# FFT filter and soft mixture of experts on one core: sign changes, row softmax, column maximum and first combine transposes placed elsewhere

## The chip, the cores and the metric

The kernel runs on one core of a Trainium2 chip. The metric is the device time of one execution in microseconds (us). The core has TensorE (PE in the profile; its weight loads are PEld), VectorE (DVE), ScalarE (ACT), GpSimd (POOL) and SyncE (SP, which here issues every DMA). Each engine works through a queue of its own in order, and waits at the head of that queue until what the next instruction needs is there.

## The reference

Two parts, one after the other. First a filter in the frequency domain, over the sequence of 2496, for 8 batches of 256 channels:

```
X = np.fft.rfft(x, axis=1)                # x: (8, 2496, 256)
Y = X * (filt_r + 1j * filt_i)[None]
y = np.fft.irfft(Y, n=2496, axis=1)
```

Then a soft mixture of experts over all 19968 tokens (8 experts, 4 slots each, hidden size 1024). It uses a softmax over tokens (down a column) to fill the 32 slots, and a softmax over slots (along a row) to give the slots' outputs back:

```
logits = x @ phi                          # (19968, 32)
d = softmax(logits, axis=0)               # per slot, over the tokens
slot_input = d.T @ x                      # (32, 256)
slot_out[e] = relu(slot_input[e] @ w1[e]) @ w2[e]
c = softmax(logits, axis=1)               # per token, over the slots
out = c @ slot_out
```

## The kernel before, in words

The transform of length 2496 is split into 39 x 64. For a batch b, eleven **s1 units** (`s1_unit`, L317) take the first transform. Each multiplies a tile of x with a table in three matmuls (L324); to keep precision x is split into a high part `xh` (ACT, L313) and a low part `xl` (POOL, L314). ACT copies the result to `at` (L325) and SP stores it in DRAM as `a_dram` (L329, L331, L332). Ten **x units** per batch (`x_unit`, L348) load it back in another layout as `ash` (L345), do the second transform (PE, L355) and multiply with the filter: DVE forms `yt` and `t2` with the tables `fr_t` and `fi_t` (L368, L369), and two half-size additions finish the complex product, L371 on DVE (on POOL for the last two batches) and L372 on POOL. Ten **t units** per batch (`t_unit`, L374) transpose the product (L380), copy it to `y` (ACT, L382), and matmul it with phi (L393) for the logits in the frequency domain, `lt` (L400). Batch 0 goes another way at the front: `first_unit` (L274) and `turn_ash` (L290) keep it on the chip.

The loop over 80 slots (L739, ten per batch) traces x units, s1 units of a batch some slots ahead, and t units. When x of batch 1 is loaded, three buffers of `xt` hold it (XB = 3); a buffer is free for the next load when its split by ACT and POOL is over.

**The tables.** `load_tables(c)` (L646) loads the parts of `fr_t` and `fi_t` for two residues t and changes the sign of some column runs of `fi_t` in place, on POOL (L653). There are ten such calls. The first four (c = 0 to 3) are traced before the first unit; the other six come in the first six slots of the loop. There are 29 sign changes: 11 in the first four calls, 18 in the other six.

**The chain of a group.** Two batches make a group g (0 to 3). When its last t unit is traced, `chain(g)` (L414) starts. It turns the logits back to the token domain (L444 to L491), takes the maximum of each slot over the group's tokens (L485, L498) in `cmax`, transposes that (L501), reduces it (L503), puts it on a diagonal `dg` (L505) and spreads it over all partitions with a matmul against `ones` (L508). This gives `m_run`. Then come the exponentials of the column softmax (L522, L523), their transform back to frequencies (L538 to L572), the sum of the exponentials `z` (L583, added in L593 or L598 as `z_ins`), and the sum over tokens `s` (80 matmuls, L604, added in L614 or L618). Last in program order is the **row softmax**: maximum along the rows `rm` (two DVE reductions, L626), subtraction and exponential in place (L630 on DVE, L631 on ACT), row sums `r_all` (L638) and their reciprocal (L640, L641). Groups 0 and 1 then store the exponentials to DRAM (`c_dram`, L644), since groups 0 to 2 share one buffer; they are read back near the end (L791).

**The order of work.** The program is traced in this order, but a list scheduler sets each engine's queue: it takes what is ready first by its own model of the times, and program order decides only among what is ready. So the row softmax, last in program order, may be issued long before `z`. `tc.issue_after(ins)` holds that back: what the block traces on `ins`'s engine is queued behind `ins`, without waiting for it to finish. In the kernel before, L620 does so for group 3 only. Group 2 is special: it is stopped before its `z` (L579) and its `s` matmuls are queued at given points of group 3's chain.

**The end.** After group 3, `psi` (L800, four matmuls) and `sit` (L802) give the slot inputs; then the experts (L865 to L891), and the combine. `combine(pos)` (L814) multiplies the exponentials with the reciprocal sums on POOL (`c1`, L826, and `cq`, L828 to L833), transposes them on PE (`ct`, L837, L840, L841) and splits them in two parts (L811 on ACT, L812 on DVE). The first one, `combine(0)`, is queued on PE behind `psi` (L854). It takes its PSUM tiles from the pool `ps_c`, which has two buffers and also holds `psi`; later ones use `ps_t`. The output matmuls (L918), the copies (L927) and the stores (L944) follow.

Of the kernel before, what the change touches and what calls it, by code (L numbers as in the profile page):

```python
# [9 lines left out]
F32 = mybir.dt.float32  # L10
F32R = mybir.dt.float32r
AF = mybir.ActivationFunctionType
ALU = mybir.AluOpType
AX = mybir.AxisListType
# [9 lines left out]
KR = PK * N1  # L24
# [11 lines left out]
SLOTS = NE * SPE  # L36
GROUPS = ((0, 1), (2, 3), (4, 5), (6, 7))
NG = len(GROUPS)
NSPILL = 2
OUT_ORDER = (4, 5, 0, 1, 2, 3, 6, 7)  # L40
P = 128
# [7 lines left out]
XB = 3  # L49
# [122 lines left out]
def flip_runs(t):  # L172

    out = []
    for c in range(N2):
        if bin_of(t, c) > SEQ // 2:
            if out and out[-1][1] == c:
                out[-1] = (out[-1][0], c + 1)
            else:
                out.append((c, c + 1))  # L180
    return out
# [27 lines left out]
def fft_soft_moe(ctx, tc, x, fr, fi, phi, w1, w2, cst, w1q, out):  # L209
    nc = tc.nc  # L210
    pe, dve, act, pool_e, sp = nc.tensor, nc.vector, nc.scalar, nc.gpsimd, nc.sync

    const = ctx.enter_context(tc.tile_pool(name="const", bufs=1))
# [14 lines left out]
    phi_t = const.tile([P, 2, SLOTS], F32, name="phi_t")  # L228
    r_all = const.tile([KR, NG, 4 * NH], F32, name="r_all")
    s_run = const.tile([P, DIM + 1], F32, name="s_run")  # L230
    cmax = const.tile([KR, SLOTS], F32, name="cmax")
    ones = const.tile([SLOTS, P], F32, name="ones")
    m_run = [const.tile([P, SLOTS], F32, name=f"m_run{i}") for i in range(NG)]

    def C(name, lo=0, hi=None):
        o, rows, cols = OFF[name]
        hi = cols if hi is None else hi
        return cst_t[0:rows, o + lo : o + hi]

    ident = C("id")  # L240

    def open_pool(name, bufs, side):
        cm = tc.tile_pool(name=name, bufs=bufs, side=side, reuse_waits="tile")
        return cm, cm.__enter__()
# [5 lines left out]
    warm_ins = dve.memset(warm, 0.0)  # L250
    with tc.issue_after(warm_ins.ins):
        nc.vector.memset(ones, 1.0)
    x0_cm, x0p = open_pool("x0p", 6, "left")
    tabs_cm, tabs = open_pool("tabs", 1, "right")
    prod_cm, prod = open_pool("prod", 2, "right")
# [148 lines left out]
    lgs = {}  # L404

    mark = {}

    def behind(g, n):

        if g != NG - 2:  # L410
            return nullcontext()
        return tc.issue_after(mark[g + 1, sum(n >= k for k in HELD)])

    def chain(g):  # L414
        bs = GROUPS[g]
        wk = late_pool[0] if g == NG - 1 else work
# [13 lines left out]
        def psum(shape, name):  # L430
            pool, tag = banks[turn[0] % len(banks)]
            turn[0] += 1
            return pool.tile(shape, F32, tag=tag, name=name)
# [36 lines left out]
        cm = wk.tile([KR, 3, SLOTS], F32, tag="cm", name=f"cm_{g}", bufs=1)  # L470
# [10 lines left out]
        for s0 in range(0, NH, SA):  # L481
# [4 lines left out]
                out=cm[:, s0 // SA, :],  # L486
                in_=pv[:, 0:n].rearrange("s a (x e) -> s e (a x)", e=SLOTS),
                axis=AX.X,
                op=ALU.max,
# [4 lines left out]
        nch = -(-NH // SA)  # L494

        NX = 2 * nb * NH
        lgf = lg_t.rearrange("s a h b e -> s (a h b) e")
        dve.tensor_reduce(out=cmax, in_=cm[:, 0:nch].rearrange("s c e -> s e c"), axis=AX.X, op=ALU.max)  # L498
        m_new, m_old = m_run[g], m_run[g - 1]
        pm = psum([SLOTS, KR], f"mt_{g}")  # L500
        mark[g, 1] = pe.transpose(pm, cmax, ident[0:KR, 0:KR]).ins  # L501
        mx = wk.tile([SLOTS, 1], F32, tag="mx", name=f"mx_{g}", bufs=1)
        dve.tensor_reduce(out=mx, in_=pm, axis=AX.X, op=ALU.max)  # L503
        dg = wk.tile([SLOTS, SLOTS], F32, tag="dg", name=f"dg_{g}", bufs=1)
        dve.tensor_scalar(out=dg, in0=ident[0:SLOTS, 0:SLOTS], scalar1=mx, scalar2=None, op0=ALU.mult)  # L505
        yield
        pmb = psum([P, SLOTS], f"mb_{g}")
        mark[g, 2] = pe.matmul(pmb, ones, dg, start=True, stop=True).ins  # L508
# [51 lines left out]
        for t0 in range(0, HT, SA):  # L560
# [10 lines left out]
            if t0 == 0:  # L571
                dve.tensor_scalar(  # L572
                    out=dd[:, 0, 0], in0=dd[:, 0, 0], scalar1=C("wh"), scalar2=None, op0=ALU.mult
# [12 lines left out]
        if g > 0:  # L586
# [6 lines left out]
            z_ins = dve.scalar_tensor_tensor(  # L593
                out=s_run[:, DIM:], in0=s_run[:, DIM:], scalar=alc, in1=pz, op0=ALU.mult, op1=ALU.add
            )
        else:
            alc = None
            z_ins = dve.tensor_copy(s_run[:, DIM:], pz)  # L598
        pss = psum([P, DIM], f"s_{g}")
        for b2, b in enumerate(bs):  # L600
            for t in range(NT):
                j = t % 4
                with behind(g, b2 * NT + t):
                    pe.matmul(  # L604
                        pss[32 * j : 32 * j + 32, :],
                        dd[:, t % HT, t // HT, b2, :],
                        ys[b, t // 2][:, t % 2, :],
                        start=(b2 == 0 and t < 4),
                        stop=(b2 == nb - 1 and t >= NT - 4),
                    )  # L610
                if t % 8 == 7:
                    yield
        if g > 0:
            s_ins = dve.scalar_tensor_tensor(  # L614
                out=s_run[:, 0:DIM], in0=s_run[:, 0:DIM], scalar=alc, in1=pss, op0=ALU.mult, op1=ALU.add
# [1 line left out]
        else:  # L617
            dve.tensor_copy(s_run[:, 0:DIM], pss)  # L618

        with tc.issue_after(z_ins.ins) if g == NG - 1 else nullcontext():  # L620
            rm = wk.tile([KR, NX], F32, tag="rm", name=f"rm_{g}", bufs=1)
            rs = r_all[:, g, 0:NX]
            step = NX // 2
            for x0 in range(0, NX, step):
                sl = slice(x0, x0 + step)
                dve.tensor_reduce(out=rm[:, sl], in_=lgf[:, sl], axis=AX.X, op=ALU.max)  # L626
        rmb = rm.rearrange("s (x o) -> s x o", o=1).broadcast_to([KR, NX, SLOTS])
        for x0 in range(0, NX, step):
            sl = slice(x0, x0 + step)
# [6 lines left out]
        for x0 in range(0, NX, step):  # L636
            sl = slice(x0, x0 + step)
# [8 lines left out]
    def load_tables(c):  # L646
        lo, hi = 2 * c, 2 * c + 2
        sp.dma_start(fr_t[:, lo:hi], fr.rearrange("q (t h c) -> q t h c", h=2, c=64)[:, lo:hi])
        sp.dma_start(fi_t[:, lo:hi], fi.rearrange("q (t h c) -> q t h c", h=2, c=64)[:, lo:hi])
        for t in range(lo, hi):  # L650
            for c0, c1 in flip_runs(t) if t else ():
                sl = fi_t[:, t, :, c0:c1]
                pool_e.tensor_scalar(out=sl, in0=sl, scalar1=-1.0, scalar2=None, op0=ALU.mult)  # L653

    CPB = NT // 2
    NS = BATCH * CPB
# [23 lines left out]
    if WM:  # L680
        pw = ps_c.tile([P, P], F32, tag="c", name="warm_up")
        for k in range(WM):
            pe.matmul(pw, warm, warm, start=True, stop=True)
    tabs_next = iter(range(CPB))
    load_tables(next(tabs_next))
    sp.dma_start(phi_t, phi.rearrange("(h q) e -> q h e", q=P))
    for k in range(XB):
        next_x()
        load_tables(next(tabs_next))
# [49 lines left out]
    for n in range(NS + LT):  # L739
# [21 lines left out]
        if n >= LT:  # L761
            b, c = divmod(n - LT, CPB)
# [36 lines left out]
    for dh in range(2):  # L799
        psi_ins = nc.tensor.matmul(psi[:, dh, :], s_run[:, dh * P : (dh + 1) * P], repz, start=True, stop=True)  # L800
# [48 lines left out]
    def new_st(pos):  # L849
        pool = tail if pos % SB < 2 else late_pool[-1]  # L850
        return pool.tile([P, 2, SQ + P], F32R, tag="st", name=f"st_{pos}", bufs=2)

    sts = {pos: new_st(pos) for pos in range(2)}
    with tc.issue_after(psi_ins.ins):  # L854
        combine(0)

    po = ps_s1.tile([P, DIM], F32, tag="s1", name="slot_out")
# [73 lines left out]
    for pos in range(BATCH):  # L931
        off = SQ * pos % P
        for m in range((off + SQ) // P):
            cols.append((sts[pos], m * P))
            g, n = nout[0], len(cols)
# [49 lines left out]
```

## Time and profile before

| what | value |
|---|---|
| median of 3 runs (lowest to highest) | 385.86 us (382.42 to 387.18) |
| the profiled execution's own time | 384.92 us |
| its span, first to last instruction | 382.8 us |
| mean granted TensorE clock | 0.974 |
| busy: PE, PEld, DVE, ACT, POOL | 349.9, 281.8, 264.2, 209.6, 213.5 us |
| DMA: moved, mean rate | 103.57 MB, 271 GB/s |

The profiled execution is 2.1 us longer than its span; that part lies around the span and is not touched here. A busy PE in this profile is not PE at its peak, since matmuls overlap and their ends are modelled. So the stretches count in which PE, or another engine, is shown idle, and what ended that idle time. "TensorE clock" is the share of the full clock that was granted.

### The profile page before, as it was taken

The page shows a single profiled execution, that of the slowest core. Times are in us where ns is not written, and L with a number is a line of the kernel's source. Part 1 is how long each engine was busy: PE and PEld are TensorE (multiplying, and loading weights), DVE is VectorE, ACT ScalarE, POOL GpSimd, SP SyncE. Part 2 cuts the span into 40 slices and gives each one's busy share as a digit, 9 for nine tenths or more (in the row PEclk, how much of TensorE's full clock was granted, in tenths as well). Part 3 has the DMA queues.
Part 4 walks back from the last instruction along what each step waited for, and adds up shares of the span by engine and source line. Part 5 has one row for each costly group of instructions (what it writes and reads, how often), then busy time and mean ns, then how long its engine had stood idle before and what let it go on. Part 6 is the DMA issues. An engine that isn't in the chain of part 4 may idle for free.

```text
span 382.8 us, 10537 instructions
## 1 busy us (share of the span) xinstructions
PE 349.9 (91%) x4111; PEld 281.8 (74%) x4111; DVE 264.2 (69%) x444; ACT 209.6 (55%) x415; POOL 213.5 (56%) x258
## 2 busy tenths in 40 slices
PE   8998969999999899999999999999989999999920
PEld 8896758888888677888887869888666534788820
DVE  2486716969798995588799837899745741677740
ACT  3757656786557864664896624336443330566730
POOL 0499966998678586585699707556640002434000
PEclk9999979999999999999999999999999999999985
DMA  7998899999879799695887835352499996699996
GB/s 245 374 281 277 224 319 281 322 310 364 299 204 293 244 303 275 197 287 139 273 276 243 264 110 174 110 129 84 145 309 380 384 383 174 241 377 413 412 419 284
DMA packets 53523, 103.57 MB, mean 271 GB/s; under 512 B 5391, under 2 KB 25999, under 8 KB 51171
## 3 DMA queue, kind: packets, MB, share of 16 engines
q1 hardware_dynamic: 53475, 102.92, 80.1%
q8 instruction: 32, 0.52, 0.5%
q14 instruction: 16, 0.13, 0.1%
HBM read 62.78 MB, written 40.12 MB: 269 GB/s over the span
## 4 chain that ended last, share of the span: by engine, by line
PE 66%; DMA 10%; DVE 9%; POOL 5%; issue 3%; ACT 2%; SPq 1%; DVEq 0%; ACTq 0%; POOLq 0%
PE x L355 14%; PE s L324 10%; PE t L380 8%; PE out L918 6%; PE s L604 5%; DMA xt<-in_x 4%; PE l L393 4%; PE v L457 3%; PE lg L484 3%; DMA out<-ob 2%; PE dd L563 2%; DMA a_dram<-at 2%; POOL xl L314 2%; PE o L882 2%; PE h L865 2%
## 5 line engine op out<-in xcount | busy, mean ns | idle before, releaser
L314 POOL TENSOR_TENSOR xl<-xt,xh 117x512 fp32r<-117x512 f32 x77 | 105.5, 1381 | 26.9 <-ACT xh L313 20.7
L355 PE MATMUL x<-cst_t,ash 128*128 128x128 f32 x640 | 87.9, 281 | 3.7 <-DMA ash<-a_dram 1.1
L355 PEld LDWEIGHTS x<-cst_t,ash 128*128 128x128 f32 x640 | 81.3, 195 | 9.8 <-issue 2.8
L372 POOL TENSOR_TENSOR yt<-yt,t 128x256 f32<-128x256 f32 x80 | 67.7, 850 | 15.5 <-DVE t L369 15.0
L368 DVE TENSOR_TENSOR yt<-x,fr_t 128x512 f32<-128x512 f32 x80 | 54.6, 682 | 28.3 <-PE l L393 17.8
L382 ACT COPY y<-t 128x512 f32<-128x512 f32 x80 | 46.7, 591 | 37.0 <-PE t L380 36.5
L313 ACT CAST xh<-xt 117x512 fp32r<-117x512 f32 x77 | 47.5, 624 | 21.0 <-DMA xt<-in_x 9.8
L369 DVE TENSOR_TENSOR t<-x,fi_t 128x512 f32<-128x512 f32 x80 | 54.2, 678 | 2.5 <-POOL yt L372 2.4
L325 ACT COPY at<-s 120x512 f32<-120x512 f32 x77 | 45.3, 590 | 13.3 <-PE s L324 11.3
L380 PE MATMUL t<-cst_t,yt 128*128 128x128 f32 x320 | 49.3, 278 | 1.1 <-POOL yt L372 0.6
L371 DVE TENSOR_TENSOR yt<-yt,t 128x256 f32<-128x256 f32 x60 | 47.6, 809 | 0.6
L380 PEld LDWEIGHTS t<-cst_t,yt 128*128 128x128 f32 x320 | 38.2, 143 | 12.3 <-issue 5.2
L324 PE MATMUL s<-xh,w1h 117*120 117x512 f32 x77 | 36.1, 469 | 3.6 <-ACT at L325 3.0
L826 POOL TENSOR_TENSOR c<-cl,r_all 117x352 f32<-117x352 f32 x8 | 6.2, 798 | 50.4 <-DMA cl<-c_dram 40.6
L324 PE MATMUL s<-xl,w1h 117*120 117x512 f32 x77 | 33.0, 428 | 0.8 <-POOL xl L314 0.8
L324 PE MATMUL s<-xh,w1l 117*120 117x512 f32 x77 | 31.0, 402 | 0.0
L371 POOL TENSOR_TENSOR yt<-yt,t 128x256 f32<-128x256 f32 x20 | 15.6, 779 | 26.9 <-DVE t L369 20.6
L918 PE MATMUL out<-so_h,st 32*128 32x256 f32 x312 | 27.3, 307 | 1.0 <-ACT so_h L894 0.5
L927 ACT COPY ob<-out 128x512 f32<-128x512 f32 (+1 forms) x42 | 21.9, 560 | 11.3 <-PE out L918 8.3
L927 DVE COPY ob<-out 128x512 f32<-128x512 f32 (+1 forms) x42 | 25.2, 647 | 3.8 <-PE out L918 2.1
L918 PE MATMUL out<-so_l,st 32*128 32x256 f32 x312 | 25.3, 284 | 0.0
L918 PEld LDWEIGHTS out<-so_h,st 32*128 32x128 f32 x312 | 20.0, 183 | 4.4 <-DVE ob L927 1.2
(112 smaller groups left out, 522.7 us busy)
## 6 DMA issues: line engine op xcount, KB each, us to landing
out<-ob SPq DMA_DIRECT2D x18, 1024.0 KB, 8.4
xt<-in_x SPq DMA_DIRECT2D x35, 512.0 KB, 4.8
ash<-a_dram SPq DMA_DIRECT2D x70, 256.0 KB, 4.3
a_dram<-at SPq DMA_DIRECT2D x70, 240.0 KB, 4.1
w<-in_w SPq DMA_DIRECT2D x64, 256.0 KB, 5.3
xt<-in_x SPq DMA_DIRECT2D x18, 256.0 KB, 5.1
c_dram<-lg SPq DMA_DIRECT2D x2, 643.5 KB
cl<-c_dram SPq DMA_DIRECT2D x2, 643.5 KB
```

What stands on the lines that cost most here:

```text
L313: act.copy(xh, xs)
L314: pool_e.tensor_tensor(out=xl, in0=xs, in1=xh.bitcast(F32), op=ALU.subtract)
L324: pe.matmul(ps, w, xx, start=(n == 0), stop=(n == 2))
L355: pe.matmul(ps[:, 2 * k + dh].rearrange("q r c -> q (r c)"), ash[:, k, dh * P : (dh + 1) * P], C("b"), start=True, stop=True,)
L368: dve.tensor_tensor(out=yt, in0=ps, in1=frv, op=ALU.mult)
L369: dve.tensor_tensor(out=t2, in0=ps[:, :, ::-1, :], in1=fiv, op=ALU.mult)
L371: add.tensor_tensor(out=yt[:, :, 1, :], in0=yt[:, :, 1, :], in1=t2[:, :, 1, :], op=ALU.add)
L372: pool_e.tensor_tensor(out=yt[:, :, 0, :], in0=yt[:, :, 0, :], in1=t2[:, :, 0, :], op=ALU.subtract)
L380: pe.transpose(pt[:, k, dh, :], yt[:, c % 2, 2 * k + dh].rearrange("q r c -> q (r c)"), ident)
L382: act.copy(y, pt.rearrange("k p h d -> k p (h d)"))
L918: last_mm[0] = nc.tensor.matmul(prs[k][:, mm, :], st[q, n % 2, c0 : c0 + P], (so_h, so_l)[n // 2][q, :], start=(n == 0), stop=(n == 3),).ins
L927: copied[k % 2] = copy(ob[:, nm * k : nm * (k + 1), :], prs[k]).ins
```

## The change

Four edits.

- The sign changes of `fi_t` leave POOL: those of the first four calls (c <= 3) go to DVE, as the same instruction; those of the other six go to ACT, as a copy with scale -1.
- The row softmax of groups 0 and 1 is queued behind the group's `z_ins` on DVE, as that of group 3 was already. Group 2's is left free as before.
- The column maximum works on full tiles: `cmax` has 128 columns instead of 32, the transposed tile `pm` 128 rows, and `ones` and `dg` 128 rows. `cmax` and `dg` are now allocated once and set to zero at the start.
- The PE instructions of `combine(0)` are queued behind the last `s` matmul instead of behind `psi`. `last_s[0]` holds the last L604 matmul traced.

```diff
-    cmax = const.tile([KR, SLOTS], F32, name="cmax")
-    ones = const.tile([SLOTS, P], F32, name="ones")
+    cmax = const.tile([KR, P], F32, name="cmax")
+    dg = const.tile([P, SLOTS], F32, name="dg")
+    ones = const.tile([P, P], F32, name="ones")
...
         nc.vector.memset(ones, 1.0)
+        nc.vector.memset(cmax, 0.0)
+        nc.vector.memset(dg, 0.0)
...
-        dve.tensor_reduce(out=cmax, in_=cm[:, 0:nch].rearrange("s c e -> s e c"), axis=AX.X, op=ALU.max)
+        dve.tensor_reduce(out=cmax[:, 0:SLOTS], in_=cm[:, 0:nch].rearrange("s c e -> s e c"), axis=AX.X, op=ALU.max)
...
-        pm = psum([SLOTS, KR], f"mt_{g}")
+        pm = psum([P, KR], f"mt_{g}")
...
-        dve.tensor_reduce(out=mx, in_=pm, axis=AX.X, op=ALU.max)
-        dg = wk.tile([SLOTS, SLOTS], F32, tag="dg", name=f"dg_{g}", bufs=1)
-        dve.tensor_scalar(out=dg, in0=ident[0:SLOTS, 0:SLOTS], scalar1=mx, scalar2=None, op0=ALU.mult)
+        dve.tensor_reduce(out=mx, in_=pm[0:SLOTS], axis=AX.X, op=ALU.max)
+        dve.tensor_scalar(out=dg[0:SLOTS], in0=ident[0:SLOTS, 0:SLOTS], scalar1=mx, scalar2=None, op0=ALU.mult)
...
-                    pe.matmul(
+                    last_s[0] = pe.matmul(
...
-                    )
+                    ).ins
...
-        with tc.issue_after(z_ins.ins) if g == NG - 1 else nullcontext():
+        with tc.issue_after(z_ins.ins) if g != NG - 2 else nullcontext():
...
-                pool_e.tensor_scalar(out=sl, in0=sl, scalar1=-1.0, scalar2=None, op0=ALU.mult)
+                if c <= XB:
+                    dve.tensor_scalar(out=sl, in0=sl, scalar1=-1.0, scalar2=None, op0=ALU.mult)
+                else:
+                    act.activation(sl, sl, AF.Copy, scale=-1.0)
...
-    with tc.issue_after(psi_ins.ins):
+    with tc.issue_after(last_s[0]):
         combine(0)
```

More of the change, by code (lines that the diff above doesn't have):

```diff
@@ L406, in fft_soft_moe @@
     mark = {}
+    last_s = [None]
     def behind(g, n):
```

## The prediction

> **What bounds the kernel now.** I read the page first, then the busy times by stretch, then the chain that ended last, then the waits of the stretches where PE stands.
>
> ```profile
> PE 349.9 (91%) x4111; PEld 281.8 (74%) x4111; DVE 264.2 (69%) x444; ACT 209.6 (55%) x415; POOL 213.5 (56%) x258
> ```
>
> PE is busy in 91% of the span, no other engine above 69%. What PE has to do is hardly touched, so a gain can only come from PE's pauses and from stretches with a low clock. Busy time by stretch (start:end, length, then busy time and count of PE, PEld, DVE, ACT, POOL, granted clock, DMA share, GB/s):
>
> ```profile
> 12.00:20.00 8.00, 7.05 (x56) 6.23 (x55) 3.38 (x5) 5.77 (x10) 4.84 (x8) 1.00 1.04 366
> 20.00:28.00 8.00, 8.00 (x62) 7.33 (x61) 7.21 (x12) 4.18 (x8) 8.00 (x16) 1.00 0.90 266
> 28.00:36.00 8.00, 7.60 (x49) 5.82 (x47) 5.26 (x8) 6.52 (x13) 8.00 (x18) 1.00 0.88 306
> 36.00:44.00 8.00, 6.63 (x67) 5.28 (x68) 4.67 (x7) 4.67 (x9) 8.00 (x9) 1.00 0.70 200
> 44.00:54.00 10.00, 6.77 (x37) 4.87 (x36) 4.98 (x7) 6.96 (x13) 10.00 (x10) 0.91 0.95 290
> 54.00:60.00 6.00, 6.00 (x28) 5.30 (x27) 0.00 (x0) 1.48 (x3) 1.65 (x2) 0.59 0.98 338
> 60.00:115.00 55.00, 55.00 (x567) 47.47 (x567) 46.79 (x72) 37.67 (x74) 44.92 (x42) 1.00 0.90 295
> ```
>
> From 20 to 54 us POOL works without a pause, while PE loses 0.40 + 1.37 + 3.23 = 5.0 us from 28 to 54. Then PE runs at a clock of 0.59 for 6 us, which costs another 6 x 0.41 = 2.5 us. From 60 us on PE has no pause for 55 us. So the start is where time can be had: 7.5 us at most, and POOL is the full engine there. The DMA engines, though, are at 0.70 to 1.04 themselves. What the start waits for in the end is in the chain (start, length, what):
>
> ```profile
> 45.25 3.20 DMA a_dram<-at
> 48.54 4.51 DMA ash<-a_dram
> 53.18 3.75 PE x L355 x16
> ```
>
> Batch 1 must be stored and loaded back before its x units, and its last store leaves at 45.25.
>
> **The sign changes.** The rows of POOL's 29 sign changes (least, median, greatest ns; first and last start) and what POOL waited for before them; then the SP queue's waits up to 60 us and PE's from 12 to 54 us:
>
> ```profile
> L653 POOL TENSOR_SCALAR fi_t<-fi_t x29: 222/357/513, 13.4 to 35.9; 128x64 f32<-128x64 f32 x9, 128x4 f32<-128x4 f32 x2, 128x60 f32<-128x60 f32 x2, 128x50 f32<-128x50 f32 x2
> ```
>
> ```profile
>   DMA fi_t<-in_fi: 13.0, 1
> ```
>
> ```profile
> SPq L329 <- ACT at L325: 8.5, 7, 2.5
> SPq L271 <- POOL xl L314: 3.4, 3, 2.6
> ```
>
> ```profile
> PE s L324 <- ACT at L325: 3.0, 4, 1.1
> ```
>
> At the median POOL is freed of 29 x 0.357 = 10.4 us, all of it ahead of batch 1's last splits. SP waits 8.5 us for `at` and 3.4 us for `xl`, with the next x loads queued behind. So the splits, the buffers of x and the loads come forward together. POOL allows 10.4 us, PE has 7.5 to give, and the transfers set a third limit: from 20 to 54 us they are busy for 0.90 x 8 + 0.88 x 8 + 0.70 x 8 + 0.95 x 10 = 29.3 of 34 us. The same bytes at the share of 0.95 seen from 44 to 54 take 29.3 / 0.95 = 30.9 us: 3.1 us earlier. I take 3.1 us, since the transfers are the nearest limit, and half of the low clock's 2.5 us, 1.2, because the pause of PE in front of it shrinks but need not vanish. Together 4.3 us.
>
> What the receivers pay. The nearest row for an ACT sign change, of at most 64 columns, is a copy of 128 columns, and the nearest for DVE is the scaling of `dd`, of 64:
>
> ```profile
> L400 ACT COPY lt<-l 128x128 f32<-128x128 f32 x1 | 0.3, 266 | 0.2 <-PE l L393 0.2
> ```
>
> ```profile
> L572 DVE TENSOR_SCALAR dd<-dd,cst_t x4: 255/1022/1276, 144.1 to 299.1; 128x64 f32<-128x64 f32 x4
> ```
>
> ACT: at most 18 x 0.266 = 4.8 us. From 20 to 36 us it is free for 3.82 + 1.48 = 5.3 us, which covers them; without that cover PE, which waits for `at` already (3.0 us), would lose up to 4.8 us more. DVE: 11 at 0.255 is 2.8 us, and at 1.022 it is 11.2 us. It has 4.62 us free from 12 to 20 us and 0.79 from 20 to 28. The one at 299 us, where POOL does nothing, is the short one. With POOL eased I take 0.4 each (4.4 us, covered), and keep 11.2 us for the range: 11.2 - 5.4 = 5.8 us on the path. The term is **-4.3**, from -7.5 to +5.8.
>
> A rule speaks against this edit. The Trainium skill, page "GPSIMD Engine Reference", section "Key points", says that GpSimd shares its SBUF interfaces with VectorE and contends with DVE instructions in a two-port mode or with two SBUF inputs. By it each DVE sign change beside a split goes at the long end, and the start would not gain but lose. The row of L572 bears it out as to the spread; whether eleven fall beside splits no run here shows yet.
>
> **Row softmax behind z.** PE's waits from 115 to 136 us (group 0) and from 186 to 207 us (group 1):
>
> ```profile
> PE x L355 <- PE x L355: 1.0, 1, 1.0
> PE x L355 <- PE t L380: 0.6, 1, 0.6
> PE t L380 <- DVE yt L371: 0.5, 1, 0.5
> ```
>
> ```profile
> PE s L324 <- POOL xl L314: 0.8, 2, 0.5
> ```
>
> 2.1 + 0.8 = 2.9 us in all. The longest one, on DVE and then on PE:
>
> ```profile
> 127.36 1.04 DVE L630 TENSOR_TENSOR lg<-lg,rm 117x704 f32<-117x704 f32 x1
> 128.33 0.68 DVE L369 TENSOR_TENSOR t<-x,fi_t 128x512 f32<-128x512 f32 x1
> ```
>
> ```profile
> 129.11 1.13 PE L355 MATMUL x<-cst_t,ash 128*128 128x128 f32 x8 [0.98 <-PE x L355]
> ```
>
> The row softmax's L630 holds DVE until 128.40, the multiplication L369 behind it frees the PSUM buffer at 129.01, and PE goes on at 129.11. Behind z there is a hole for this work, because PE runs only `s` there:
>
> ```profile
> 154.08 0.42 DVE L618 COPY s_run<-s 128x256 f32<-128x256 f32 x1 [4.18 <-PE s L604]
> ```
>
> ```profile
> 224.91 0.48 DVE L614 SCALAR_TENSOR_TENSOR s_run<-s_run,alc,s 128x256 f32<-128x256 f32 x1 [4.13 <-PE s L604]
> ```
>
> ```profile
> L630 DVE TENSOR_TENSOR lg<-lg,rm 117x704 f32<-117x704 f32 x8 | 7.8, 986 | 0.0
> L626 DVE TENSOR_REDUCE rm<-lg 117x22 f32<-117x704 f32 x8 | 7.0, 880 | 0.8 <-ACT lg L491 0.8
> L638 DVE TENSOR_REDUCE r_all<-lg 117x22 f32<-117x704 f32 x8 | 6.9, 872 | 0.1
> ```
>
> Per group 2 x 0.880 + 2 x 0.986 = 3.7 us go into 4.1 to 4.2 idle ones. The sums, 2 x 0.872 = 1.7 us, come after `s` among the next multiplications; if they are not hidden there they cost 1.7 us. Behind the waiting `rm` only its own chain is queued. The stores to `c_dram` move with it on SP:
>
> ```profile
> L644 SPq DMA_DIRECT2D c_dram<-lg x2: 353/384/416, 132.4 to 203.4; - x2
> ```
>
> ```profile
> 243.23 0.86 PE lg L484 x2
> ```
>
> They would leave at about 155 and 226, and the loads queued behind them on SP wait if the exponentials are late. Group 1's buffer is written again only after group 2's L484, at 243, so 17 us are left for that store. Not all of the 2.9 us hangs on row softmax (group 1's waits are for POOL), so I take some two thirds: **-2.0**, from -2.9 to +1.7.
>
> **Full tiles for the maximum.** The work stays as it is in count; the weights get 128 columns.
>
> ```profile
> L508 PEld LDWEIGHTS mb<-dg,ones 32*128 32x128 f32 x8 | 1.2, 182 | 1.0 <-issue 0.8 <-DVE yt L368 0.2
> ```
>
> 0.8 us of idle stands before the spreading matmuls, of four groups. I take **-0.2**, from -0.8 to 0, as the neighbours hide most of it. The two memsets at the start find DVE waiting for the first table. The Trainium skill, "TensorEngine Tiling (Array Packing)", "Key Properties", says that a change of tiling mode drains TensorE. By it the full 0.8 us would go where the neighbours are full tiles, and the forecast would be 378.8.
>
> **First combine transposes.** DVE, then PE around psi, the two halves of the split as groups, and the first matmul of the experts:
>
> ```profile
> 304.37 0.48 DVE L614 SCALAR_TENSOR_TENSOR s_run<-s_run,alc,s 128x256 f32<-128x256 f32 x1 [0.52 <-PE s L604]
> 305.57 0.23 DVE L802 COPY sit<-psi 128x64 f32<-128x64 f32 x1 [0.72 <-PE psi L800]
> ```
>
> ```profile
> 304.90 0.63 PE L800 MATMUL psi<-repz,s_run 128*128 128x32 f32 x4 [0.60 <-DVE s_run L614]
> 305.37 0.60 PE L837 MATMUL ct<-cst_t,c 117*128 117x117 f32 x4
> ```
>
> ```profile
> L812 DVE TENSOR_TENSOR st<-ct,st 128x468 fp32r<-128x468 f32 x8 | 5.2, 645 | 1.9 <-ACT st L811 1.9
> ```
>
> ```profile
> L811 ACT CAST st<-ct 128x468 fp32r<-128x468 f32 x8 | 4.5, 564 | 1.7 <-PE ct L837 1.7
> ```
>
> ```profile
> 306.32 3.64 PE L865 MATMUL h<-w,sit 128*32 128x512 f32 x32
> ```
>
> Now L865 starts 0.5 us after `sit` is ready (305.80), because the transposes lie between, from 305.37 on. Put ahead they fill the 0.60 us in which PE waits for `s_run`; as all of them take 0.95 us, psi slips by up to 0.35. So at best the 0.5 us goes. But `ps_c` has two buffers: if the transposes take both, psi waits until the first is split by ACT and DVE, 0.56 + 0.65 = 1.2 us. The two ends nearly cancel, and I take **0.0**, from -0.5 to +1.2.
>
> **Sum.** -4.3 - 2.0 - 0.2 + 0.0 = -6.5 us on the profiled execution's 384.9 us (span 382.8 and 2.1 around it): 378.4. The median of the runs is 0.9 us above that execution, so **379.4 us**, 1.7% below 385.86.
>
> **Rivals.** (A) *The transfers hold the start.* Batch 1 comes no earlier, since the DMA share is 0.95 to 1.04 in the stretches on either side; against it stands 0.70 from 36 to 44 us. Only -2.2 is left: 383.7. (B) *POOL was the only limit.* PE's pauses and the low clock go in full, -7.5, and row softmax gives -2.9: with -0.5 from the rest -10.9, so 375.0. For it: POOL at 8.00 of 8 from 20 on. Against: the DMA share. (C) *Row softmax only moves.* Its subtractions meet POOL's splits in the new place too, and the sums delay the next batch: +1.7 in place of -2.0, so 383.1. (D) *DVE's sign changes become the bound*, the slower side: in DVE's queue, from 12 to 28 us, each waits for POOL and takes 1.02 us; the first multiplications of batch 0 come 5.8 us late and PE, in order, with them. With -2.2 from the rest +3.6: 389.5. It decides from (4.62 + 0.79) / 11 = 0.49 us for each sign change on. This is the outcome that the page on GpSimd would have.
>
> **How the numbers follow.** Forecast 0.41, A 0.18, B 0.21, C 0.12, D 0.08. About 2% is what a measurement of this kernel can tell from no change: below 378.1 is faster, above 393.6 slower. All of B and a third of the forecast's share lie below 378.1: 0.21 + 0.13 = 0.34; of D a quarter above 393.6, 0.02; the rest, 0.64, within. The range of 373.5 to 387.0 takes in B, the forecast, A and C and leaves out most of D; the forecast's own range is 376.5 to 382.
>
> **What would show it.** Right: POOL has pauses between 20 and 44 us, the last store of batch 1 leaves before 43 us, its first x unit starts at about 50 and the clock from 54 to 60 us is well above 0.59. L626 of groups 0 and 1 starts right behind L598 and L593, the idle 4.1 us before L618 and L614 is gone, and no wait of PE near 129 us names a buffer held by L369. DVE's sign changes take below 0.49 us each, and L865 starts no later behind L614 than now (306.32 - 304.37 = 1.95 us). Wrong: x units of batch 1 again at 53 us or later, sign changes on DVE or ACT with long waits ahead of them, or new pauses of PE at 155 and 226 us.

## The result, and the profile after

| | before | after |
|---|---|---|
| median of 4 runs each, side by side (lowest to highest) | 386.52 us (382.42 to 388.82) | 374.35 us (373.21 to 374.38) |
| ratio, with 95% interval | | 0.971 (0.963 to 0.979) |
| span of the profiled execution | 382.8 us | 372.4 us |
| mean granted clock | 0.974 | 0.982 |

Faster by 2.9%; the ratio compares only the executions in the faster of the two states that executions of a kernel fall into, so it is not quite the quotient of the medians. The forecast of 379.4 us had the right sign and the right places, and somewhat over half of the size; 374.35 us lies inside the range, at rival B's 375.0. In the changed kernel's profile line numbers are 3 to 6 higher (L653 became L657 on DVE and L659 on ACT, L355 is L358, L626 is L629).

The busy times of the page, after:

```profile
PE 345.0 (93%) x4111; PEld 280.0 (75%) x4111; DVE 276.2 (74%) x457; ACT 212.1 (57%) x433; POOL 199.9 (54%) x229
```

PE's share rises from 91% to 93% with the same 4111 matmuls. The start, by stretch, after:

```profile
20.00:28.00 8.00, 8.00 (x60) 7.25 (x59) 7.97 (x16) 7.04 (x25) 5.65 (x7) 1.00 0.98 320
28.00:36.00 8.00, 8.00 (x63) 7.09 (x61) 7.74 (x11) 7.12 (x17) 8.00 (x9) 1.00 1.02 342
36.00:44.00 8.00, 8.00 (x76) 6.56 (x75) 4.72 (x9) 6.35 (x13) 6.84 (x6) 1.00 0.88 284
44.00:54.00 10.00, 8.52 (x71) 6.74 (x74) 4.93 (x7) 6.17 (x13) 8.42 (x9) 1.00 0.97 304
54.00:60.00 6.00, 6.00 (x66) 5.36 (x65) 5.62 (x11) 3.96 (x8) 5.40 (x6) 1.00 1.04 377
```

POOL now has pauses (5.65 of 8, 6.84 of 8, 8.42 of 10). PE loses 1.48 us from 28 to 54 where it lost 5.0, and the clock stays at 1.00 throughout, where it stood at 0.91 from 44 to 54 us and at 0.59 from 54 to 60 us before. The chain of waits, after, at the hand-over to batch 1:

```profile
43.32 0.20 PE t L383 x2
43.52 4.32 DMA ash<-a_dram
47.84 0.14 issue
47.98 1.13 PE x L358 x8
```

The first x unit of batch 1 starts at 47.98 us, 5.2 earlier than the 53.18 of before. It still waits for the load of `ash`, but that load left behind a `t` unit of PE at 43.5, no longer behind a late store at 45.25.

DVE around the `z` of group 0, after (start, length):

```profile
139.08 0.14 DVE L601 COPY s_run<-z 128x1 f32<-128x1 f32 x1
139.15 1.66 DVE L629 TENSOR_REDUCE rm<-lg 117x22 f32<-117x704 f32 x2
140.73 1.68 DVE L633 TENSOR_TENSOR lg<-lg,rm 117x704 f32<-117x704 f32 x2
142.47 1.69 DVE L641 TENSOR_REDUCE r_all<-lg 117x22 f32<-117x704 f32 x2
144.07 0.42 DVE L621 COPY s_run<-s 128x256 f32<-128x256 f32 x1
```

L629 stands right behind L601, and the idle 4.18 us in front of the addition of `s` is gone. Even the sums (L641) fit in. All that is left of PE's waits from 105 to 140 us, after:

```profile
PE t L383 <- ACT at L328: 0.7, 1, 0.7
```

No wait there names a buffer that DVE holds.

### The profile page after: what moved, and what is told of

Its sections match the earlier page's. It is cut to its first block, busy times and chain, and to the rows that moved or that the text cites. A ratio compares the mean times of both kernels' runs of the same rounds, so it can differ in the third digit from the quotient of the medians.

```text
span 372.4 us, 10529 instructions
## 1 busy us (share of the span) xinstructions
PE 345.0 (93%) x4111; PEld 280.0 (75%) x4111; DVE 276.2 (74%) x457; ACT 212.1 (57%) x433; POOL 199.9 (54%) x229
## 4 chain that ended last, share of the span: by engine, by line
PE 73%; DVE 12%; DMA 6%; issue 3%; ACT 1%; SPq 1%; POOL 0%; DVEq 0%; ACTq 0%; POOLq 0%
PE x L358 16%; PE s L327 13%; PE t L383 8%; PE out L924 6%; PE s L607 5%; PE l L396 5%; PE v L461 3%; PE lg L488 3%; DMA out<-ob 2%; DVE yt L371 2%; PE dd L566 2%; DVE t L372 2%; PE o L888 2%; DVE d L525 2%; PE h L871 2%
## 5 line engine op out<-in xcount | busy, mean ns | idle before, releaser
L317 POOL TENSOR_TENSOR xl<-xt,xh 117x512 fp32r<-117x512 f32 x77 | 101.8, 1328 | 57.5 <-ACT xh L316 56.8
L358 PE MATMUL x<-cst_t,ash 128*128 128x128 f32 x640 | 87.6, 277 | 1.6 <-DMA ash<-a_dram 1.5
L358 PEld LDWEIGHTS x<-cst_t,ash 128*128 128x128 f32 x640 | 80.2, 191 | 8.6 <-issue 5.1
L316 ACT CAST xh<-xt 117x512 fp32r<-117x512 f32 x77 | 47.6, 623 | 26.8 <-PE s L327 15.5
L374 DVE TENSOR_TENSOR yt<-yt,t 128x256 f32<-128x256 f32 x60 | 55.3, 934 | 1.0
L383 PEld LDWEIGHTS t<-cst_t,yt 128*128 128x128 f32 x320 | 38.1, 141 | 12.3 <-POOL yt L375 3.6
L327 PE MATMUL s<-xl,w1h 117*120 117x512 f32 x77 | 32.1, 417 | 0.0
L396 PE MATMUL l<-yt,phi_t 128*32 128x128 f32 x640 | 23.2, 276 | 0.1
```

The lines of the kernel that those rows point to most:

```text
L316: act.copy(xh, xs)
L317: pool_e.tensor_tensor(out=xl, in0=xs, in1=xh.bitcast(F32), op=ALU.subtract)
L327: pe.matmul(ps, w, xx, start=(n == 0), stop=(n == 2))
L358: pe.matmul(ps[:, 2 * k + dh].rearrange("q r c -> q (r c)"), ash[:, k, dh * P : (dh + 1) * P], C("b"), start=True, stop=True,)
L374: add.tensor_tensor(out=yt[:, :, 1, :], in0=yt[:, :, 1, :], in1=t2[:, :, 1, :], op=ALU.add)
L383: pe.transpose(pt[:, k, dh, :], yt[:, c % 2, 2 * k + dh].rearrange("q r c -> q (r c)"), ident)
```

## The experiments

The table gives the start of the first x unit of batches 1 and 3, and the time from the latter to the first x unit of batch 7, in each kernel's profile. The first two columns show the start alone. The third contains row softmax of groups 0 and 1 and nothing of the start. The ratio is against the kernel before on the same chip, with its 95% interval; the times that follow each text of what was expected are medians.

| kernel | x of batch 1 | x of batch 3 | batch 3 to 7 | ratio |
|---|---|---|---|---|
| before | 53.18 | 112.00 | 136.76 | 1 |
| combine_only | 52.80 | 111.02 | 136.73 | 1.004 (1.000 to 1.008) |
| max_only | 52.24 | 110.63 | 136.88 | 1.003 (0.999 to 1.007) |
| rows_only | 53.18 | 111.37 | 133.59 | 0.989 (0.982 to 0.997) |
| flips_only | 47.59 | 103.97 | 136.74 | 0.987 (0.979 to 0.995) |
| no_flips_at_all | 47.20 | 103.80 | 135.64 | 0.977 (0.969 to 0.984) |
| act_flips | 47.65 | 103.80 | 136.75 | 0.979 (0.972 to 0.986) |
| dve_flips | 50.08 | 106.28 | 136.72 | 0.982 (0.975 to 0.989) |
| pool_flips_thrice | 65.36 | 124.60 | 135.74 | 1.029 (1.020 to 1.037) |
| after | 47.98 | 105.06 | 133.63 | 0.971 (0.963 to 0.979) |
| after_pool_flips | 53.77 | 111.39 | 133.65 | 0.987 (0.977 to 0.997) |
| after_free_rows | 48.78 | 105.45 | 136.73 | 0.980 (0.971 to 0.989) |
| flips_rows | 48.00 | 104.68 | 133.62 | 0.971 (0.964 to 0.977) |
| combine_first | 47.80 | 104.70 | 133.69 | 0.970 (0.963 to 0.977) |

Theory after the result: the sign changes on POOL were the limit of the whole start, and moving the row softmax gives more than PE's waits had shown; the other two edits do nothing. Rivals: the two large edits need each other; the receivers pay; the gain is only that the list scheduler draws up other queue orders.

### Each edit alone

**flips_only**, the sign changes alone:

```diff
-                pool_e.tensor_scalar(out=sl, in0=sl, scalar1=-1.0, scalar2=None, op0=ALU.mult)
+                if c <= XB:
+                    dve.tensor_scalar(out=sl, in0=sl, scalar1=-1.0, scalar2=None, op0=ALU.mult)
+                else:
+                    act.activation(sl, sl, AF.Copy, scale=-1.0)
```

> The kernel before with the sign changes moved to DVE and ScalarE, nothing else. Theory (POOL held the start): the first x unit of batch 1 starts near 48 us instead of 53.2, the low clock from 54 to 60 us is gone, and the time falls by 6.5 to 8 us, to about 379 us. Rival (the start was as fast in the changed kernel only because the scheduler happened to order things well): the first x unit of batch 1 at 51 us or later, and less than 4 us gained.

Measured: 377.37 against 383.68 us, 6.3 less, just under the 6.5 to 8 expected. Batch 3 starts at 103.97 us. The five kernels with the sign changes once on POOL start it at 110.63 to 112.00 (mean 111.28), the five with the sign changes of the change at 103.97 to 105.45 (mean 104.77). So the edit is worth **6.5 us**, and the kernel that was profiled as before was itself 0.7 us later than its like.

**rows_only**, the row softmax alone:

```diff
-        with tc.issue_after(z_ins.ins) if g == NG - 1 else nullcontext():
+        with tc.issue_after(z_ins.ins) if g != NG - 2 else nullcontext():
```

> The kernel before with the row softmax of groups 0 and 1 queued behind z, nothing else. Theory (it stood on DVE in front of work that PE waited for): the start is as before, PE gains about 3 us between the maximum and the s matmuls of group 0 and about 0.7 us at group 1, the time falls by 2.5 to 4 us, to about 383 us. Rival (row softmax only moves its load): within 1 us of before, with new pauses of PE behind the s matmuls.

Measured: 380.23 against 383.68 us. The third column is 133.59 to 133.69 in all five kernels with this edit and 136.7 to 136.9 in seven of the nine without it: **3.1 us**. The other two, no_flips_at_all and pool_flips_thrice, have 135.6 and 135.7 with the row softmax in its old place, so another order of the queues can be worth 1 us here. From the first x unit of batch 7 to the first output matmul it is 76.8 to 77.0 us in the five, 77.3 in before and max_only and up to 80.1 in the others. That is perhaps another 0.4, **3.5 us** in all, but it isn't shown: combine_only, with the queues of before, takes 78.9 there.

Where that comes from: one row for the same work of PE, some 877 matmuls around group 0, of before and then of rows_only.

```profile
120.20:198.50 78.30, 75.79 (x877) 62.63 (x876) 64.82 (x104) 51.87 (x105) 55.51 (x48) 1.00 0.82 254
```

```profile
119.70:195.30 75.60, 74.90 (x876) 62.50 (x875) 67.69 (x101) 49.43 (x99) 51.47 (x47) 1.00 0.81 259
```

PE is idle for 2.51 us of the first and 0.70 of the second, 1.8 less. A further 0.9 us lies inside PE's busy time, 75.79 against 74.90 for the same matmuls at the same clock. No list of waits shows that part. Most of it hangs on the pauses too. In the profile neighbouring x matmuls start some 0.11 us apart (eight in 0.89 us) and last 0.27, so each overlaps the next by 0.16 us, and a pause costs that overlap besides its idle time. The first stretch has five pauses of PE of over 0.1 us, the second one: 4 x 0.16 = 0.6 us. What the remaining 0.3 us is stays open.

**max_only**, full tiles for the column maximum alone:

```diff
-    cmax = const.tile([KR, SLOTS], F32, name="cmax")
-    ones = const.tile([SLOTS, P], F32, name="ones")
+    cmax = const.tile([KR, P], F32, name="cmax")
+    dg = const.tile([P, SLOTS], F32, name="dg")
+    ones = const.tile([P, P], F32, name="ones")
...
-        pm = psum([SLOTS, KR], f"mt_{g}")
+        pm = psum([P, KR], f"mt_{g}")
```

> The kernel before with the column maximum on full tiles, nothing else. Theory: nothing, within 0.5 us of before, and the idle time of 0.8 us in front of the spreading matmuls stays. Rival (a change of tiling mode costs PE a pause here): 0.8 us faster, and that idle time is gone.

Measured: 384.78 against 383.68 us; the interval of the ratio holds 1, so no gain and no loss is shown. The weight loads of the spreading matmuls in max_only and in the changed kernel:

```profile
L510 PEld LDWEIGHTS mb<-dg,ones 128*128 128x128 f32 x8 | 1.3, 189 | 0.7 <-issue 0.6
```

```profile
L511 PEld LDWEIGHTS mb<-dg,ones 128*128 128x128 f32 x8 | 1.2, 188 | 1.0 <-issue 0.8 <-DVE yt L371 0.2
```

Before, 0.8 us of "issue" stood in front of them; with full tiles it is 0.6 and 0.8. So it wasn't a change of tiling mode that caused it, and the drain that the Trainium skill tells of ("TensorEngine Tiling (Array Packing)", "Key Properties") has no price that these rows show.

**combine_only**, the combine edit alone:

```diff
-    with tc.issue_after(psi_ins.ins):
+    with tc.issue_after(last_s[0]):
         combine(0)
```

> The kernel before with the first combine transposes queued behind the last s matmul, nothing else. Theory: psi still goes first on PE, as in the changed kernel, so every queue is the same as before and the time too (this also shows how far two builds with the same queues lie apart). Rival (the transposes go first and psi waits for a buffer): the first expert matmul 1 us later behind the last s matmul.

Measured: 384.69 against 383.68 us, no difference. The edit permits an earlier place but gives none: `psi` is earlier in program order, and the scheduler still issues it first. After, PE and DVE:

```profile
293.96 0.48 DVE L617 SCALAR_TENSOR_TENSOR s_run<-s_run,alc,s 128x256 f32<-128x256 f32 x1 [0.53 <-PE s L607]
294.50 0.63 PE L806 MATMUL psi<-repz,s_run 128*128 128x32 f32 x4 [0.60 <-DVE s_run L617]
294.96 0.60 PE L843 MATMUL ct<-cst_t,c 117*128 117x117 f32 x4
295.92 1.50 PE L871 MATMUL h<-w,sit 128*32 128x512 f32 x12
```

The transposes still follow `psi`, and L871 starts 295.92 - 293.96 = 1.96 us behind L617, against 1.95 before. This kernel's queues are those of the kernel before on every engine, so its 1.0 us beside before in the second column is what two executions of one program differ by.

### Is it POOL's time, the receivers, or the order?

**no_flips_at_all**, no sign changes:

```diff
-                pool_e.tensor_scalar(out=sl, in0=sl, scalar1=-1.0, scalar2=None, op0=ALU.mult)
+                pass
```

> The kernel before without its 29 sign changes of fi (that part of the computation is left out, so the filter's imaginary table keeps its stored signs). Theory, POOL's sign changes were what the start waited for and the receivers hide them: about as fast as the kernel with the sign-change edit alone, -5 to -8 us against before, first x unit of batch 1 at 47 to 48 us (before: 53.2), full clock from 44 to 60 us. Rival, the receivers DVE and ACT pay for a good part of what POOL is spared: -9 to -11 us and the first x unit of batch 1 at 45 us or earlier. Rival, the edit gains only by the other queue orders that the list scheduler draws up: this kernel has orders of its own, so anything from 0 to -8 us, without tie to POOL's load. Rival, the transfers hold the start: 47 to 48 us as in the first case, with the DMA share at 0.95 or more from 20 to 54 us and POOL with pauses.

Measured: 377.53 against 386.45 us. Batch 1 starts at 47.20 and batch 3 at 103.80, 1.0 us earlier than the mean of those where DVE and ACT do the work (104.77). So the receivers hide most of it. By the medians the gain is 8.9 us, more than the 5 to 8 expected; but 1.1 us of that stands in the third column, long after the sign changes, and the rival's start at 45 us or earlier didn't come. The sign of its last rival did: from 20 to 54 us the DMA share is 0.97 and POOL has pauses (busy for 30.46 of 34 us). So with POOL eased the transfers may hold the start at 47 us, or PE, busy for 33.34 of the same 34 us; no run separates these two.

**pool_flips_thrice**, each sign change three times on POOL:

```diff
+                for _ in range(3):
-                pool_e.tensor_scalar(out=sl, in0=sl, scalar1=-1.0, scalar2=None, op0=ALU.mult)
+                    pool_e.tensor_scalar(out=sl, in0=sl, scalar1=-1.0, scalar2=None, op0=ALU.mult)
```

> The kernel before with each sign change done three times on POOL (three times is one time in value). It adds 58 instructions of some 0.36 us, 20.7 us, to POOL in the first 50 us. Theory, POOL is the limit there: the first x unit of batch 1 moves from 53 us to 65 to 74 us, PE's pauses and the low clock grow, and the whole is 10 to 20 us slower. Rival, the transfers are the limit and POOL only follows them: at most 5 us slower and the first x unit of batch 1 before 58 us. Rival, only the scheduler's orders matter: no tie to the 20.7 us.

Measured: 397.33 against 386.45 us. The group of sign changes, and the start by stretch:

```profile
L654 POOL TENSOR_SCALAR fi_t<-fi_t 128x64 f32<-128x64 f32 (+14 forms) x87 | 26.4, 332 | 12.8 <-DMA fi_t<-in_fi 12.8
```

```profile
28.00:36.00 8.00, 4.50 (x24) 3.37 (x25) 3.40 (x5) 3.87 (x7) 8.00 (x17) 0.97 0.79 263
36.00:44.00 8.00, 6.51 (x30) 4.20 (x28) 4.08 (x5) 4.09 (x8) 8.00 (x19) 0.82 0.61 160
44.00:54.00 10.00, 7.78 (x64) 6.11 (x63) 4.57 (x7) 3.85 (x7) 10.00 (x25) 0.83 0.63 199
54.00:60.00 6.00, 4.11 (x30) 3.35 (x28) 3.09 (x5) 2.86 (x5) 6.00 (x11) 1.00 0.68 203
```

POOL is full, while every other engine has pauses and the transfers fall to 160 GB/s beside it. 58 x 0.332 = 19.3 us more on POOL make batch 1 start 12.3 us later (53.0, the mean of the five, to 65.36) and batch 3 13.3 us later.

**dve_flips** and **act_flips**, all 29 sign changes on one of the receivers:

```diff
-                pool_e.tensor_scalar(out=sl, in0=sl, scalar1=-1.0, scalar2=None, op0=ALU.mult)
+                dve.tensor_scalar(out=sl, in0=sl, scalar1=-1.0, scalar2=None, op0=ALU.mult)
```

```diff
-                pool_e.tensor_scalar(out=sl, in0=sl, scalar1=-1.0, scalar2=None, op0=ALU.mult)
+                act.activation(sl, sl, AF.Copy, scale=-1.0)
```

> The kernel before with all 29 sign changes on DVE (the same instruction on another engine) and nothing else changed. Theory: DVE has room, at 0.18 to 0.4 us each that is 5 to 12 us beside other work; first x unit of batch 1 at 47 to 49 us and -4 to -7 us against before. Rival (the predicted case D on a larger scale: each DVE sign change beside a split on POOL waits and takes some 1 us): 29 us on a DVE that has about 8 us free from 12 to 36 us, so +5 to +15 us, with the mean of the sign changes above 0.49 us.

> The kernel before with all 29 sign changes on ACT as copies with scale -1, and nothing else changed. Theory: 29 x 0.24 = 7 us on ACT, which has 7.5 us free from 12 to 36 us; first x unit of batch 1 at 47 to 49 us, -4 to -8 us against before. Rival, ACT's copies of the first transform (SP waited 8.5 us for them in the kernel before) come later and pass that on to the stores: first x unit of batch 1 at 50 us or later, -3 us or less.

Measured against 386.45 us: 379.79 on DVE, 378.77 on ACT. Their groups, in dve_flips and act_flips (busy, mean ns):

```profile
L653 DVE TENSOR_SCALAR fi_t<-fi_t 128x64 f32<-128x64 f32 (+16 forms) x29 | 11.1, 442 | 2.4 <-DMA fi_t<-in_fi 2.3
```

```profile
L653 ACT ACTIVATE fi_t<-fi_t 128x64 f32<-128x64 f32 (+16 forms) x29 | 4.8, 235 | 0.4 <-DMA fi_t<-in_fi 0.4
```

ACT takes all 29 at 0.235 us each without a trace in the start (103.80, as with no sign changes at all). On DVE they take nearly twice that and cost 2.5 us of the start (106.28), which still leaves 5.0 of gain; batch 1 comes at 50.08, 1.1 us later than the theory allowed, but the mean of 0.44 us is below the rival's 0.49.

What follows: batch 1's start goes with POOL's load (47.2 to 50.1 with none, 53.0 with 10 us, 65.4 with 29 us), in six different orders of the queues, since the scheduler draws up its own for each of these edits. The clock goes with it too: from 20 to 60 us its mean is 0.91 to 0.96 in the six kernels with sign changes on POOL, and 1.00 in the eight others. That speaks against luck of the order. It doesn't exclude that a part of the gain is the order: no kernel here had the old order with POOL eased, and that stays open.

### The edits together

**after_pool_flips** and **after_free_rows** take one of the two large edits back out of the changed kernel:

```diff
-                if c <= XB:
-                    dve.tensor_scalar(out=sl, in0=sl, scalar1=-1.0, scalar2=None, op0=ALU.mult)
-                else:
-                    act.activation(sl, sl, AF.Copy, scale=-1.0)
+                pool_e.tensor_scalar(out=sl, in0=sl, scalar1=-1.0, scalar2=None, op0=ALU.mult)
```

```diff
-        with tc.issue_after(z_ins.ins) if g != NG - 2 else nullcontext():
+        with tc.issue_after(z_ins.ins) if g == NG - 1 else nullcontext():
```

> The changed kernel with the 29 sign changes back on POOL, the other three edits kept. Theory, the edits act in different stretches and add up: the start is that of the kernel before (first x unit of batch 1 at 52 to 53.5 us, clock below 0.9 from 54 to 60 us), and the whole is 6 to 8 us slower than the changed kernel, -3 to -5 us against before, as with the row-softmax edit alone. Rival, the edits need each other (row softmax gains only when POOL is eased, since its subtractions meet the splits): no faster than 1 us against before.

> The changed kernel with the row softmax of groups 0 and 1 free again, the other three edits kept. Theory: 2.5 to 4 us slower than the changed kernel, -6 to -8.5 us against before, with PE's pauses of 115 to 136 us back (some 2 us or more of waiting there) and the hole of about 4 us on DVE before s_run is added to, back as well. Rival, with POOL eased the old place of the row softmax costs nothing: within 1 us of the changed kernel, -9.5 us or more against before.

Measured against 384.74 us: 380.10 and 378.48. Each puts back the loss of its own column in the table and leaves the other alone: 111.39 and 133.65 for the one, 105.45 and 136.73 for the other. In after_free_rows PE's pause around group 0 is back; its row and that of the changed kernel:

```profile
115.00:130.00 15.00, 12.76 (x151) 10.38 (x149) 15.00 (x19) 10.81 (x24) 10.35 (x8) 1.00 0.82 276
```

```profile
115.00:130.00 15.00, 14.31 (x197) 12.61 (x196) 14.03 (x21) 9.27 (x22) 9.48 (x10) 1.00 0.82 275
```

DVE is full for all 15 us and PE stands for 2.24 of them, against 0.69. The edits don't need each other, and they add up: 6.5 + 3.1 = 9.6, or 10.0 with the 0.4 that isn't shown, against the 10.4 between the two profiled spans. The medians of the first table lie further apart, 12.2 us; the kernel before spread over 6.4 us in its four runs there, and no experiment accounts for the rest.

**flips_rows** leaves the two small edits out, **combine_first** carries out what the fourth only permits, on top of the changed kernel:

```diff
+    combine(0)
     zr = const.tile([P, 1], F32, name="zr")
...
-    with tc.issue_after(last_s[0]):
-        combine(0)
```

> The kernel before with the sign changes and the row softmax moved, without full tiles for the maximum and without the combine edit. Theory: those two bring nothing, so this is as fast as the changed kernel, -10 to -12 us against before. Rival: full tiles (or the two extra memsets) gain or lose more than 1 us here, which single edits on the kernel before did not show.

> The changed kernel with combine(0) traced ahead of psi instead of only being allowed there: its transposes are queued on PE inside group 3's chain, some 8 us before psi, and psi is followed at once by the first matmul of the experts. The prediction's bounds for this step: -0.5 us, if the transposes only lie between psi and the experts now, to +1.2 us, if they hold both buffers of ps_c until ACT and DVE have split them. Theory: L617's end to the first matmul of the experts shrinks by 0.3 to 0.5 us from 1.96 us, and the time stays within 1 us of the changed kernel, -9.5 to -12 us against before. Rival: the splits sit on ACT and DVE in the middle of group 3's chain, which PE waits for, and delay s of group 3 by 1 us or more.

Measured against 384.74 us: 373.89 and 373.93, as fast as the changed kernel. The end of group 3 in combine_first:

```profile
293.94 0.48 DVE L617 SCALAR_TENSOR_TENSOR s_run<-s_run,alc,s 128x256 f32<-128x256 f32 x1 [0.53 <-PE s L607]
294.48 0.63 PE L855 MATMUL psi<-repz,s_run 128*128 128x32 f32 x4 [0.60 <-DVE s_run L617]
295.42 2.78 PE L871 MATMUL h<-w,sit 128*32 128x512 f32 x24 [0.32 <-DVE sit L857]
```

The transposes now run ahead inside group 3's chain, and L871 starts 1.48 us behind L617: 0.48 us sooner, the whole of the 0.5 that lay between. L617 comes no later than in the changed kernel (293.94 to 293.96). That is a gain of 0.1% at most, below what the times can tell; no version here beats the changed kernel by a measurable amount.

## Why the prediction was right in sign and short in size

**The start: -4.3 predicted, -6.5 measured.** The mechanism was right: POOL got pauses, and splits, stores and loads came forward together. Of the 6.5 us, 5.0 lie ahead of the first x unit of batch 1 (a mean of 53.0 us for the five kernels with the sign changes once on POOL, 48.0 for the five with those of the change) and 1.5 between it and batch 3, where most of the low clock was. The prediction had 3.1 and 1.2.

*The low clock, 1.2 us, "half of the low clock's 2.5 us, because the pause of PE in front of it shrinks but need not vanish".* All of it went. Before, in steps of 2 us:

```profile
48.00:50.00 2.00, 0.86 (x4) 0.46 (x3) 1.40 (x1) 1.97 (x5) 2.00 (x2) 1.00 0.86 286
50.00:52.00 2.00, 0.98 (x4) 0.46 (x3) 0.00 (x0) 1.74 (x4) 2.00 (x4) 1.00 0.89 279
52.00:54.00 2.00, 0.94 (x5) 0.85 (x5) 0.00 (x0) 1.10 (x2) 2.00 (x2) 0.53 1.00 356
54.00:56.00 2.00, 2.00 (x11) 2.00 (x11) 0.00 (x0) 0.00 (x0) 0.37 (x1) 0.50 0.99 326
56.00:58.00 2.00, 2.00 (x8) 1.60 (x8) 0.00 (x0) 0.59 (x1) 0.49 (x1) 0.50 1.03 377
58.00:60.00 2.00, 2.00 (x12) 1.70 (x10) 0.00 (x0) 0.89 (x2) 0.79 (x1) 0.76 0.93 312
```

The clock was withheld for 2 x (0.47 + 0.50 + 0.50 + 0.24) = 3.4 us in all, that is 6.8 us at 0.50; the prediction began to count at 54 us. But until 53.18 PE stood waiting for `ash`, and a low clock takes nothing from an engine that stands. From there on it ran slower: 16 x matmuls take 3.75 us, against 2.02 at 1.00 in no_flips_at_all. From 53.18 to 59.0 us that is 5.8 us at 0.50, a loss of up to 2.9 us by the clock's share, but from batch 1 to batch 3 only 1.7 us come out in the two profiles (58.82 to 57.08), 1.5 in the means. What takes up the rest in the changed kernel is open. So the 1.2 us were close to what came out, by luck: the halving stood for a low clock that stays in part, and none of it stayed, though PE still waits for `ash` at the hand-over (1.5 us after, 1.1 before).

*The transfers as "the nearest limit", 3.1 us.* This is the step that failed: batch 1 came 5.2 us earlier in the two profiles, and not 3.1. From 20 us to the first x unit of batch 1, before, after and without sign changes:

```profile
20.00:53.18 33.18, 28.19 (x208) 22.48 (x207) 22.12 (x33) 22.25 (x42) 33.18 (x50) 0.98 0.86 265
```

```profile
20.00:47.98 27.98, 26.50 (x210) 22.82 (x208) 24.33 (x38) 23.50 (x58) 24.47 (x23) 1.00 0.96 312
```

```profile
20.00:47.20 27.20, 26.54 (x208) 22.63 (x206) 21.63 (x33) 21.48 (x41) 24.73 (x23) 1.00 0.96 318
```

33.18 x 265 = 8.79 MB before and 27.98 x 312 = 8.73 MB after: the same bytes. The share did rise to 0.96, as the prediction had it. What it took as fixed, the transfers' busy time, wasn't: for these bytes it fell from 28.5 to 26.9 us. Nor is a share of 0.95 a ceiling on the rate: the rows that gave it had 290 GB/s at 0.95 and, from 12 to 20 us, 366 GB/s at 1.04, and at the latter the bytes would have needed only 24 us. On PE, the idle time of these rows falls from 4.99 to 1.48 us, 3.5 less, and the busy time from 28.19 to 26.50, 1.7 less for nearly the same matmuls. Before, PE had seven pauses here, the last one up to the hand-over; after, that one alone. Six times the lost overlap of 0.16 us is 1.0 of the 1.7 us. After the change PE is nearly full up to the hand-over, 26.50 of 27.98 us, and the transfers are at 0.96, and which of them is the next limit isn't shown.

**The receivers** were hidden but for 1.0 us, about as forecast. ACT's 18 sign changes are within their bound. DVE's 11 fell at both ends of the range. After, least, median and greatest in ns:

```profile
L659 ACT ACTIVATE fi_t<-fi_t x18: 206/240/271, 21.5 to 30.4; 128x64 f32<-128x64 f32 x6, 128x4 f32<-128x4 f32 x2, 128x60 f32<-128x60 f32 x2, 128x50 f32<-128x50 f32 x2
L657 DVE TENSOR_SCALAR fi_t<-fi_t x11: 157/180/1302, 13.3 to 22.4; 128x64 f32<-128x64 f32 x3, 128x46 f32<-128x46 f32 x1, 128x18 f32<-128x18 f32 x1, 128x10 f32<-128x10 f32 x1
```

```profile
L657 DVE TENSOR_SCALAR fi_t<-fi_t 128x64 f32<-128x64 f32 (+8 forms) x11 | 5.1, 521 | 2.3 <-DMA fi_t<-in_fi 2.3
```

Their mean, 0.52 us, is above the 0.49 from which rival D was to decide, and the sign "below 0.49 us each" failed for four of the eleven; D still didn't come. The eleven need 11 x 0.52 = 5.7 us of DVE where 5.4 were free, so only 0.3 us of loss was due, and batch 0's first x unit at 19.24 us is within the 18.34 to 19.65 of all kernels here. D's price of 5.8 us belongs to eleven long ones, and there were four.

**Row softmax: -2.0 predicted, -3.1 to -3.5 measured**, beyond the -2.9 at which its range ended. The step that failed is the equation of the gain with PE's waits in two windows: it took "some two thirds" of 2.9 us, and 0.9 us around group 0 alone lies in PE's busy time, most of it overlap that each pause breaks. The two windows did hold the right wait, and the hole took even the sums, which had been given up to 1.7 us of cost.

**Full tiles: -0.2 predicted, nothing measured**; the idle time stayed. **Combine: 0.0 predicted, 0.0 measured**, but not because two ends cancel: the edit moves no instruction. Where the transposes really go ahead, the gain is the lower bound (-0.48), and the wait for buffers of `ps_c` that the upper bound feared doesn't come, since the splits are over long before `psi`.

**The rivals.** B, POOL as the only limit, is nearest to what happened: its terms were 7.5, 2.9 and 0.5, the measured ones 6.5, 3.1 to 3.5 and 0. That the median comes so near to its 375.0 us is in part luck, since the experiments account for 10.0 us of the 12.2 between the medians. A (the transfers hold batch 1 where it was) falls with flips_only and no_flips_at_all, where batch 1 comes at 47 to 48 us, and with pool_flips_thrice, where the transfers slow down with POOL; that they are the next limit doesn't. C (row softmax only moves) falls with rows_only. D falls with dve_flips, where even 29 sign changes on DVE leave 5.0 of the 6.5 us.

## What to carry to other kernels

Where one engine is full for a whole stretch while PE pauses and the transfers slow down beside it, take that engine for the limit until a row shows the next one at its own best rate. Don't take the transfers' busy time for fixed: here it fell by 1.6 us for the same bytes. Count a low clock only where PE has work, and look for its beginning in finer steps. PE's idle time is a lower bound on what its pauses cost, since each also breaks an overlap; comparing the time for the same matmuls shows the rest.

## What was not expected of the hardware

**DVE's sign changes are held by a running split.** POOL and DVE, after, at 15.5 us; then DVE before POOL's first split:

```profile
15.46 2.52 POOL L317 TENSOR_TENSOR xl<-xt,xh 117x512 fp32r<-117x512 f32 x2 [15.02 <-ACT xh L316]
15.49 2.52 DVE L657 TENSOR_SCALAR fi_t<-fi_t 128x64 f32<-128x64 f32 x2 [0.18 <-DMA fi_t<-in_fi]
```

```profile
13.33 0.27 DVE L657 TENSOR_SCALAR fi_t<-fi_t 128x46 f32<-128x46 f32 x2 [2.16 <-DMA fi_t<-in_fi]
```

Two splits of 1.26 us each and two sign changes of 1.26 us each, side by side; two such instructions take 0.27 us together when POOL is idle. Each long one ends 0.03 to 0.06 us behind a split. The splits lose nothing: their mean over the kernel is 1.328 us, against 1.381 before. The Trainium skill says that GpSimd shares its SBUF interfaces with VectorE and contends with DVE instructions in a two-port mode ("GPSIMD Engine Reference", "Key points"); the trace agrees that the two get in each other's way, and adds the size: three of the eleven sign changes last until the end of a split, 1.3 us in place of 0.18, the median, and a fourth 0.66 us. Which mode they run in no run here shows.

**The clock falls without a long pause.** Before, PE was busy for 1.84 of the 4 us from 48 to 52, with pauses of at most 1.14 us, and soon after 52 us the clock went to 0.50 for 6.8 us. After, one pause of 1.49 us between busy stretches left it at 1.00.
